# An attention and gated-unit backward kernel: dV and dK accumulated as their transposes, and one more row tile of dS turned by DMA

## The chip, the cores and the metric

The kernel runs on one core of a Trainium2 chip. The metric is the device time of one execution in microseconds (us), lower is better. Before the change it is 5135.07 us, the median of 3 runs (5125.85 to 5143.78).

## What is computed

The program computes the forward output of a small block and the gradients of all its inputs but one, in bf16. Cut to what matters (S = 2048 rows, D = 576, H = 32 heads of 128, F = 4608):

```python
xn = layernorm(x)
q  = (xn @ wq)                       # split in 32 heads
p  = softmax(q @ k_cache.T * 128**-0.5)      # per head, 2048 x 2048
s  = concat_heads(p @ v_cache) @ wo
g  = silu((sigmoid(xn @ w_gate) * (xn @ w_up)) @ w_down)
out = x + s * g
# outputs: out, and by jax.vjp with grad_out the gradients
# of x, k_cache, v_cache, wq, wo, w_gate, w_up, w_down
```

The change concerns the gradients of the two caches. Per head they are dV = P^T dO and dK = dS^T Q, with P the 2048 x 2048 matrix of softmax weights, dS = P * (dP - delta), and dP = dO V^T. Each result is 2048 x 128.

## The kernel before

The work runs in stages, one after the other on the one core.

- **Gate and up projections** (L292 to L334), **down projection** (L359 to L397): before the heads.
- **Heads** (L719 to L773): 32 heads, one after the other, with the next head's preparation woven into the present one. This is by far the longest stage.
- **Output projection** (L826 to L851): 16 row tiles, which read the heads' outputs back transposed (`oT`, L810).
- **Feed-forward gradients** (L879 to L946): 18 blocks of 256 columns. Each block loads `h_blk`, `a_blk`, `b_blk` (L865 to L873; the loads for block fb + 2 are issued in block fb), and in the first ten blocks one piece of the transposed down weights (`wdT`, L824).
- **Attention weight gradients** (L981 to L1016): 8 groups of 4 heads. Each group loads `onb` and `dqb` for the group after next (L975, L976), and the first five groups also load two pieces of the transposed up and gate weights (L1016).
- **dx** (L1032 to L1077): 8 blocks of 256 rows. Each makes 8 passes over chunks that are loaded transposed (`cf`, `cq`, L1042); three `cf` buffers and two `cq` buffers let the loads run ahead. The first block also loads the transposed `wq` (L92, called from L1044).

Inside a head the order is written by hand: every small piece of work gets a position (`at`, `anchor`, L427 to L431), a head is 64 positions long, and the pieces are issued in the order of their positions. A head has two halves of 32 positions. In the first, row tile qt (128 of the 2048 query rows, 16 tiles) gets its scores `sp` on TensorE at position 2 qt (`s_half`, L529), the softmax on VectorE and ScalarE (`sneg`, `Pq`), and then P's row tile is transposed (`trans_dma`, L584) into a `PT` tile for the product P V. In the second half, at 32 + 2 qt, the same goes for dP and dS (`dp_half`, L558; `dST` tiles for the product dS K). The products with the transposed tiles are `row_mm` (L593), 16 matmuls for each row tile, placed 12.1 positions after the start of their group of four (XO, XQ, L669). The transposed tiles come from one pool of 7 (NPT, L405).

A transpose goes one of two ways. By DMA: one `dma_start_transpose` on the SP queue for a whole 128 x 2048 row tile (L585). On TensorE: 16 transposing matmuls into PSUM and two copies, one by ScalarE and one by VectorE (`trans_pe`, L587, with `pe_transposes`, L500). `PE_DS = {9}` (L408) sends row tile 9 of dS, and no other, through TensorE. So a head issues 16 transposes of P and 15 of dS on the SP queue. That queue runs in order, and during the heads it carries almost nothing else. All other transfers of the stage (the head's K and V, its weight slices, and all results) are issued from GpSimd and go over the software queue q0.

dV and dK are made by `kv_mm` (L611). For each row tile and each 128 keys, the 128 x 128 piece of P (or dS) is the stationary operand and the row tile of dO (or Q) the moving one, 128 columns wide. The result piece has the keys in its partitions. A head makes dV and dK in two halves of 1024 keys, four passes in all. In each pass the 8 matmuls of a row tile lie at places that `level` (L692) spreads evenly over positions 24 to 86.7, given the other TensorE work (`load_`). Four pieces of 128 keys share a PSUM bank. A finished bank is copied by ScalarE and written by GpSimd's DMA directly to the output (L628 to L630), 1 KB per partition and transfer.

Of the kernel before, what the change touches and what calls it, by code (L numbers as in the profile page):

```python
# [9 lines left out]
bf = mybir.dt.bfloat16  # L10
f32 = mybir.dt.float32
PSUM = bass.MemoryType.PSUM
DRAM = bass.MemoryType.DRAM
P = 128
# [81 lines left out]
def kernel(  # L96
# [6 lines left out]
    nc = tc.nc  # L103
    cfg = dict(cfg or {})
    _, S, D = A_x.shape
    _, H, Sk, Dh = A_k_cache.shape
# [3 lines left out]
    NT = S // P  # L110
# [4 lines left out]
    CH = min(512, S)  # L115
# [18 lines left out]
    dram = ctx.enter_context(tc.tile_pool(name="dram", bufs=1, space=DRAM))  # L134
# [8 lines left out]
    dg_d = dram.tile([S, F], bf, name="dg_d")  # L143
    on2_d = dram.tile([S, HD], bf, name="on2_d")
    dq2_d = dram.tile([S, HD], bf, name="dq2_d")

    pers = ctx.enter_context(tc.tile_pool(name="pers", bufs=1))
    ident = pers.tile([P, P], bf, name="ident")
# [27 lines left out]
    with tc.tile_pool(name="pa", bufs=1) as pa:  # L176
# [159 lines left out]
        if True:  # L336
# [9 lines left out]
            with tc.tile_pool(name="a2h", bufs=1, reuse_waits="tile") as hp, \  # L346
# [12 lines left out]
                for sg in range(NT // SG):  # L359
# [7 lines left out]
                    for sl in range(SG):  # L367
# [36 lines left out]
    KPC = CH // P  # L404
    NSLAB, NPT = 20, 7  # L405
    STT2 = {4, 9, 14}
    PE_P = set()
    PE_DS = {9}  # L408
    with tc.tile_pool(name="ld2", bufs=2) as ld2, tc.tile_pool(name="ld1q", bufs=1) as ld1q, \
            tc.tile_pool(name="slab", bufs=NSLAB) as slabp, \  # L410
            tc.tile_pool(name="wsneg", bufs=2) as wsneg, \
# [15 lines left out]
        def at(pos, fn, *args):  # L427
            prog.append((pos, len(prog), fn, args))
# [179 lines left out]
            if after:  # L608
                at(pos + step * (GQ - 1) + width + AFTER, after)

        def kv_mm(bx, hs, slabs, rhs, half, qt, j, sink):  # L611
            i, jj = j // KPC, j % KPC
            if qt == 0 and jj == 0:
                bx.acc[i] = ps_acc.tile([P, KPC, P], f32, name="acckv", tag="acc")
            k0 = (half * 2 * KPC + j) * P
            nc.tensor.matmul(bx.acc[i][:, jj, :], lhsT=slabs[qt][:, k0:k0 + P], rhs=getattr(hs, rhs)[:, qt, :],  # L616
                             start=(qt == 0 and jj == 0), stop=(qt == NT - 1 and jj == KPC - 1))
            if qt == NT - 1 and jj == KPC - 1:
                sink(bx.acc[i], i)

        def kv(b, pos, hs, slabs, rhs, half, out_dram):
            ov = out_dram.rearrange("(p t) d -> p t d", t=NT)
            bx = Box()
            bx.acc = [None, None]

            def sink(acc, i):
                c = half * 2 + i
                kv_t = stg.tile([P, KPC, P], bf, name="kv")  # L628
                alt.copy(kv_t[:], acc[:], eng=KVE[i])
                nc.gpsimd.dma_start(ov[:, c * KPC:(c + 1) * KPC, :], kv_t[:])  # L630

            n = 2 * KPC
            for qt in range(NT):
                for j in range(n):
# [84 lines left out]
        for h in range(H):  # L719
            hs = Head(h)  # L720
            b = h * HEAD
            back = lambda x: b - HEAD + x if h else b - 14 + x / 8
            at(back(35.0), load_w, hs)
            at(back(35.1), load_kv, hs)
            for c in range(NCH):
                for i in range(DT):
                    at(back(QT_AT[0][c] + PSTEP * i), proj, hs, "QT", c, i, QT_AT[1])
                    at(b + DOT_AT[0][c] + PSTEP * i, proj, hs, "dOT", c, i, DOT_AT[1])
            at(b + WOT_AT, prep_wo, hs, "s")
            for g in range(2):  # L730
                at(back(KT_AT[g]), prep_kt, hs, g, KT_AT[2])
                at(b + DON_AT[g], prep_don, hs, g, DON_AT[2])
                at(b + VT_AT[g], prep_vt, hs, g, VT_AT[2])
                at(b + QN_AT[g], prep_qn, hs, g, QN_AT[2])
            for p in range(NT // 2):
                at(b + 4 * p + 2 + RINV_AT, s_rinv, hs, p)
                at(b + max(4 * p + 2.1 + RINV_AT, DON_AT[p // 4] + 0.5), s_scale, hs, p)
            for qt in range(NT):
                p1, p2 = b + 2 * qt, b + H1 + 2 * qt
                for hf in range(NHF):  # L740
                    anchor(p1 + hf, s_half, hs, qt, hf)
                    anchor(p2 + hf, dp_half, hs, qt, hf)
                at(p1 + EXP_AT, s_exp, hs, qt)
                if qt in PE_P:
                    for g in range(2):
                        at(p1 + 5.3 + g, trans_pe, hs.PT, hs.P, qt, "PT", g, "s")
                else:
                    at(p1 + PT_AT, trans_dma, hs.PT, hs.P, qt, "PT")
                if qt in PE_DS:
                    for g in range(2):  # L750
                        at(p2 + DST_PE[g], trans_pe, hs.dST, hs.dS, qt, "dST", g, "sv"[g])
                else:
                    at(p2 + DST_AT, trans_dma, hs.dST, hs.dS, qt, "dST")
            for g in range(NG):
# [21 lines left out]
    if True:  # L776
# [19 lines left out]
        with tc.tile_pool(name="c1b", bufs=1, side="right", reuse_waits="tile") as blk, \  # L796
# [26 lines left out]
            def load_wdT(i, k=0):  # L823
                nc.sync.dma_start_transpose(wdT_h[k][:, i, :], B_w_down[k * FH:(k + 1) * FH, dlo[i]:dlo[i] + P])  # L824
# [32 lines left out]
        with tc.tile_pool(name="b1o", bufs=2, reuse_waits="tile") as outp, tc.tile_pool(name="b1t", bufs=3, reuse_waits="tile") as tmpp, \  # L857
# [21 lines left out]
            for fb in range(F // FB):  # L879
# [45 lines left out]
                load_abh(fb + 2)  # L925
                if fb < DT * (NWD - 1):
                    load_wdT(fb % DT, 1 + fb // DT)
                for (blk_, out_, nm) in ((du_blk, out_7, "dwu"), (dg_blk, out_6, "dwg")):
                    stg_ = outp.tile([P, DL, FB], bf, name=nm)
                    for i, (d0, kd) in enumerate(dts[:DL]):  # L930
                        acc = psw.tile([P, 512], f32, name="accw", tag="tr")
                        for st in range(NT):
                            nc.tensor.matmul(acc[:kd, :FB], lhsT=xn_all[:, st, d0:d0 + kd], rhs=blk_[:, st, :],  # L933
                                             start=(st == 0), stop=(st == NT - 1))
                        alt.copy(stg_[:kd, i, :], acc[:kd, :FB])
                    for i, (d0, kd) in enumerate(dts[:DL]):
                        nc.gpsimd.dma_start(out_[d0:d0 + kd, fcols], stg_[:kd, i, :])
# [15 lines left out]
        HG = ldiv(H, 4)  # L953
        NHG = H // HG
        with tc.tile_pool(name="c2b", bufs=1, reuse_waits="tile") as blk, tc.tile_pool(name="c2s", bufs=2, reuse_waits="tile") as sb, \
                tc.tile_pool(name="c2w", bufs=1, reuse_waits="tile") as wp, tc.tile_pool(name="c2b0", bufs=1, reuse_waits="tile") as blk0, \
                tc.tile_pool(name="c2ps", bufs=2, space=PSUM, reuse_waits="tile") as ps, \
                tc.manual_schedule(engines={mybir.EngineType.SP}):
# [22 lines left out]
            for hg in range(NHG):  # L981
# [32 lines left out]
                load_hg(hg + 2)  # L1014
                for (dst, src, d0, kd) in wT_loads[2 * hg:2 * hg + 2]:
                    nc.sync.dma_start_transpose(dst[:, :, d0:d0 + kd], src[d0:d0 + kd, :])  # L1016

        SB2 = min(256, S)
        FC = ldiv(FT, 12)
        HC = ldiv(H, 16)  # L1020
        with tc.tile_pool(name="c4c", bufs=1, reuse_waits="tile") as chp, tc.tile_pool(name="c4s", bufs=2, reuse_waits="tile") as sb, \
                tc.tile_pool(name="c4w", bufs=1, reuse_waits="tile") as wp, \
                tc.tile_pool(name="c4ps", bufs=2, space=PSUM, reuse_waits="tile") as ps, \
                tc.manual_schedule(engines={mybir.EngineType.SP}):
# [3 lines left out]
            def load_wqT(k):  # L1028
                load_T_rows(nc, wqT_q[k], A_wq[:, k * HQ * P:(k + 1) * HQ * P], D)

            NSB = S // SB2
            for sbi in range(S // SB2):  # L1032
# [7 lines left out]
                for pi, (src_d, wT, k0, KC, nm) in enumerate(passes):  # L1040
                    ch = chp.tile([P, KC, SB2], bf, name=f"cq{pi % 2}" if nm == "cq" else f"cf{pi % 3}")
                    nc.sync.dma_start_transpose(ch[:], src_d[scol, k0 * P:(k0 + KC) * P])  # L1042
# [10 lines left out]
                for sl in range(nsl):  # L1053
# [21 lines left out]
                    dx = sb.tile([P, D], bf, name="dx")  # L1075
                    nc.vector.tensor_tensor(dx[:], t2[:], got[:], op=ALU.add)
                    (nc.sync if sbi == NSB - 1 else nc.gpsimd).dma_start(o1[rows, :], dx[:])  # L1077
        pc3.release()
        pc.release()

# [29 lines left out]
```

## Time and profile before

The profiled execution took 5140.72 us as a run, 5.7 us more than the median of the three; its span, from the first to the last instruction, is 5138.9 us. All other numbers below are from this execution.

| stage | from, us | to, us | PE busy | DMA share |
|---|---|---|---|---|
| heads (without their ends) | 480 | 3710 | 3165.43 of 3230 | 1.15 |
| feed-forward gradients | 3875 | 4460 | 582.22 of 585 | 0.73 |
| attention weight gradients | 4463 | 4714 | 251.00 of 251 | 0.81 |
| dx | 4715 | 5130 | 407.62 of 415 | 0.73 |

PE is TensorE. "Busy" is the union of the times in which an engine has an instruction under way. The DMA share is the time that packets took, summed over all queues and divided by 16 DMA engines; packets of different queues overlap on one engine, so the share can pass 1. The granted TensorE clock is 1.00 in the heads' stretch and 0.993 over the whole span.

Two more rows help later. Of the transfers, a DMA transpose of P lands 6.0 us after its issue in the median and one of dS 6.1 us; the q1 queue (SP) moved 719.49 MB in 2,626,976 packets and took 81.8% of the 16 engines' span, q0 (GpSimd) 285.79 MB and 19.4%. A head's own loads over q0 are K and V with 512 KB each, and its results 16 writes of 128 KB.

### The profile page before, as it was taken

The numbers are of one execution on the slowest core, as the hardware profiler recorded it, in microseconds if no ns is written. First come the engines' busy times: TensorE is split into PE (matmuls) and PEld (weight loads), VectorE is DVE, ScalarE is ACT, GpSimd is POOL, SyncE is SP. The second block draws the span as 40 slices with busy tenths as digits, with TensorE's granted clock in tenths as the row PEclk, the third lists the DMA queues.
The fourth block names the chain that finished last, engine by engine and source line by source line (L and its number), as shares of the span: only waits on it lengthen the run. The fifth ranks groups of instructions, "written<-read, shape, count | busy, mean of one in ns | idle before, by whom it ended". The sixth has DMA issues, their size and how long they took to land.

```text
span 5138.9 us, 128238 instructions
## 1 busy us (share of the span) xinstructions
PE 5018.4 (98%) x55312; PEld 3595.6 (70%) x55312; DVE 3072.1 (60%) x4821; ACT 2447.8 (48%) x3131; POOL 1481.5 (29%) x2197
## 2 busy tenths in 40 slices
PE   9999999999999999999999999999799999999999
PEld 3345777777777778777777877777657777754554
DVE  6546777777777788788778878877532222210101
ACT  5523656665666567666656666766401222100000
POOL 4322322332233233323323332332222333211000
PEclk9999999999999999999999999999999999999999
DMA  7887999999999999999999999999999776697775
GB/s 256 274 200 164 191 188 193 198 199 195 195 194 197 194 199 197 202 199 203 196 199 200 201 197 203 203 195 200 197 185 241 204 201 192 206 244 159 154 153 120
DMA packets 2712809, 1013.48 MB, mean 197 GB/s; under 512 B 2525744, under 2 KB 2648624, under 8 KB 2712240
## 3 DMA queue, kind: packets, MB, share of 16 engines
q1 hardware_dynamic: 2626976, 719.49, 81.8%
q0 software_dynamic: 85264, 285.79, 19.4%
q8 instruction: 432, 7.08, 0.6%
q14 instruction: 137, 1.12, 0.1%
HBM read 172.54 MB, written 201.00 MB: 73 GB/s over the span
## 4 chain that ended last, share of the span: by engine, by line
PE 90%; DMA 6%; DVE 2%; SPq 1%; ACT 1%; issue 1%; DVEq 0%; POOL 0%; ACTq 0%; POOLq 0%
PE acckv L616 16%; PE acc L597 16%; PE sp L537 8%; PE acc L1051 8%; PE dp L567 7%; PE accp L496 5%; PE accw L933 5%; DMA dST<-dSq 4%; PE dh L892 3%; PE acc L377 3%; PE accd L910 3%; PE g_ps L280 2%; PE acc L989 2%; PE acct L503 2%; PE u_ps L280 2%; PE accq L998 2%
## 5 line engine op out<-in xcount | busy, mean ns | idle before, releaser
L597 PE MATMUL acc<-Kn,dST 128*128 128x128 bf16 x8192 | 1087.1, 220 | 54.6 <-DMA dST<-dSq 54.5
L548 ACT ACTIVATE Pq<-sneg,nm 128x2048 bf16<-128x2048 bf16 x512 | 1024.7, 2001 | 227.5 <-DVE sneg L539 222.8
L616 PE MATMUL acckv<-dOn,Pq 128*128 128x128 bf16 x8192 | 1077.0, 220 | 0.0
L570 DVE SCALAR_TENSOR_TENSOR dSq<-dp,delta,Pq 128x1024 bf16<-128x1024 f32 x608 | 774.3, 1282 | 504.8 <-PE dp L567 500.6
L597 PE MATMUL acc<-Vn,PT 128*128 128x128 bf16 x8192 | 1051.5, 219 | 12.3 <-DMA PT<-Pq 12.3
L616 PE MATMUL acckv<-Qn,dSq 128*128 128x128 bf16 x8192 | 979.8, 219 | 0.0
L616 PEld LDWEIGHTS <-Pq 128*128 128x128 bf16 x8192 | 754.2, 98 | 227.8 <-issue 12.1
L616 PEld LDWEIGHTS <-dSq 128*128 128x128 bf16 x8192 | 742.8, 98 | 180.7
L597 PEld LDWEIGHTS <-dST 128*128 128x128 bf16 x8192 | 748.6, 98 | 169.8 <-DMA dST<-dSq 63.7
L597 PEld LDWEIGHTS <-PT 128*128 128x128 bf16 x8192 | 728.5, 98 | 104.4 <-DMA PT<-Pq 13.9
L539 DVE TENSOR_SCALAR_CACHE_REDUCE sneg<-sp,nm 128x1024 bf16<-128x1024 f32 x512 | 657.1, 1283 | 93.2 <-PE sp L537 66.2
L539 DVE TENSOR_SCALAR_CACHE_REDUCE sneg<-sp 128x1024 bf16<-128x1024 f32 x512 | 625.4, 1221 | 114.0 <-PE sp L537 101.0
L573 ACT ACTIVATE t<-dp,negdelta 128x1024 bf16<-128x1024 f32 x416 | 464.9, 1117 | 422.0 <-PE dp L567 415.7
L537 PE MATMUL sp<-KT,QT 128*128 128x512 bf16 x2048 | 612.0, 381 | 5.9 <-DVE sneg L539 5.6
L567 PE MATMUL dp<-VT,dOT 128*128 128x512 bf16 x2048 | 611.6, 380 | 0.0
L556 POOL TENSOR_TENSOR dOn<-dOn,rinv_all 128x256 bf16<-128x256 bf16 x256 | 153.8, 610 | 510.2 <-DVE dOn L42 323.3
L577 DVE TENSOR_TENSOR dSq<-t,Pq 128x1024 bf16<-128x1024 bf16 x416 | 289.6, 696 | 0.0
L1051 PEld LDWEIGHTS <-cf 128*128 128x128 bf16 x2304 | 146.0, 98 | 142.9 <-DMA cf<-dg_d 5.1
L496 PE MATMUL accp<-xnT,wq_h 128*128 128x512 bf16 x640 | 242.5, 384 | 2.3 <-ACT xnT L40 0.8
L933 PEld LDWEIGHTS <-xn_all 128*128 128x128 bf16 x2304 | 224.2, 98 | 27.8
L663 POOL DMA_DIRECT2D dq_d<-dq_n x128 | 99.1, 774 | 479.8 <-DVE dq_n L662 443.1
L1064 DVE SCALAR_TENSOR_TENSOR junk<-dxn,xn_all 128x576 f32<-128x576 f32 x16 | 12.1, 758 | 371.0 <-ACT dxn L1059 371.0
(185 smaller groups left out, 7044.2 us busy)
## 6 DMA issues: line engine op xcount, KB each, us to landing
out_dram<-kv POOLq DMA_DIRECT2D x256, 128.0 KB, 4.7
h_d<-h_row POOLq DMA_DIRECT2D x48, 384.0 KB, 2.8
a_d<-a_row POOLq DMA_DIRECT2D x48, 384.0 KB, 3.4
b_d<-b_row POOLq DMA_DIRECT2D x48, 384.0 KB, 4.5
a_blk<-a_d SPq DMA_DIRECT2D x18, 1024.0 KB, 5.9
b_blk<-b_d SPq DMA_DIRECT2D x18, 1024.0 KB, 21.6
du_d<-du_blk POOLq DMA_DIRECT2D x18, 1024.0 KB, 8.5
dg_d<-dg_blk POOLq DMA_DIRECT2D x18, 1024.0 KB, 11.5
```

Of the source, the lines that this page charges most:

```text
L496: nc.tensor.matmul(acc[:], lhsT=w[:, i, :], rhs=(srcT if i < DL else xnT)[:, i, cs], start=(i == 0), stop=(i == DL))
L537: nc.tensor.matmul(sp[:, c * CH:(c + 1) * CH], lhsT=hs.QT[:, qs], rhs=hs.KT[:, hf * HW_ + c * CH: hf * HW_ + (c + 1) * CH], start=True, st ...
L539: nc.vector.tensor_scalar(sneg[:, hf * HW_:(hf + 1) * HW_], sp[:], -SCALE, None if hf == 0 else nm[:, hf - 1:hf], op0=ALU.mult, op1=ALU.mi ...
L548: nc.scalar.activation(Pq[:], sneg[:], AF.Exp, bias=nm[:, hf:hf + 1], scale=-1.0, accum_out=hs.rs_all[:, qt:qt + 1])
L567: nc.tensor.matmul(dp[:, c * CH:(c + 1) * CH], lhsT=hs.dOT[:, qs], rhs=hs.VT[:, hf * HW_ + c * CH: hf * HW_ + (c + 1) * CH], start=True, s ...
L570: nc.vector.scalar_tensor_tensor(dSq[:, hsl], dp[:], hs.delta[:, qt:qt + 1], Pq[:, hsl], op0=ALU.subtract, op1=ALU.mult)
L573: nc.scalar.activation(t[:], dp[:], AF.Identity, bias=hs.negdelta[:, qt:qt + 1], scale=1.0)
L577: nc.vector.tensor_tensor(dSq[:, hsl], t[:], Pq[:, hsl], op=ALU.mult)
L597: nc.tensor.matmul(bx.acc[:, j, :], lhsT=T[qt][:, kt, :], rhs=getattr(hs, rhs)[:, kt, :], start=(kt == 0), stop=(kt == NT - 1))
L616: nc.tensor.matmul(bx.acc[i][:, jj, :], lhsT=slabs[qt][:, k0:k0 + P], rhs=getattr(hs, rhs)[:, qt, :], start=(qt == 0 and jj == 0), stop=(q ...
L933: nc.tensor.matmul(acc[:kd, :FB], lhsT=xn_all[:, st, d0:d0 + kd], rhs=blk_[:, st, :], start=(st == 0), stop=(st == NT - 1))
L1051: nc.tensor.matmul(accs[sl][j][:, :nn], lhsT=ch[:, kk, sl * P:(sl + 1) * P], rhs=w_[:, n0:n0 + nn], start=(pi == 0 and kk == 0), stop=(las ...
```

## The change

It does three things.

1. `kv_mm` swaps its operands. The row tile of dO or Q (128 x 128) is now stationary and 512 keys of P's or dS's row tile are moving. One matmul of 512 columns takes the place of four of 128. The PSUM bank then holds 128 (head dimension) x 512 (keys), which is a piece of dV or dK transposed. Two matmuls of a row tile and pass remain, at the places that the first and the fifth of the eight had.
2. The transposed pieces go, in the same 128 KB writes on GpSimd's queue, into two new scratch tensors in DRAM, `dkT_d` and `dvT_d`. A new helper `turn` later loads a head's 128 x 2048 scratch by a DMA transpose into a `turn` tile and writes that tile to the output, 4 KB per partition. There are 64 such pairs of transfers, all on the SP queue: two in each of the 18 feed-forward blocks, two in each of the 8 attention weight groups, and the last 12 in dx, one at a time. A call of `turn` first issues the writes of the tiles that the call before had loaded. Each of the three stages has a pool of two `turn` tiles of 4 KB per partition.
3. `PE_DS` is emptied: row tile 9 of dS is transposed by DMA like the others. The placing of dV and dK by `level` follows, as it no longer has to leave room for it.

```diff
+    dkT_d = dram.tile([H, P, S], bf, name="dkT_d")
+    dvT_d = dram.tile([H, P, S], bf, name="dvT_d")
+    turns = [(src[h], out[0, h].rearrange("(p t) d -> p t d", t=NT)) for h in range(H) for src, out in ((dkT_d, out_2), (dvT_d, out_3))]
+    turned = []
+
+    def turn(pool, n):
+        while turned:
+            nc.sync.dma_start(*turned.pop(0))
+        for _ in range(n):
+            if turns:
+                src, dst = turns.pop(0)
+                t_ = pool.tile([P, NT, P], bf, name="turn")
+                nc.sync.dma_start_transpose(t_[:], src)
+                turned.append((dst, t_[:]))
...
-    PE_DS = {9}
+    PE_DS = set()
...
-        def kv_mm(bx, hs, slabs, rhs, half, qt, j, sink):
-            i, jj = j // KPC, j % KPC
-            if qt == 0 and jj == 0:
-                bx.acc[i] = ps_acc.tile([P, KPC, P], f32, name="acckv", tag="acc")
-            k0 = (half * 2 * KPC + j) * P
-            nc.tensor.matmul(bx.acc[i][:, jj, :], lhsT=slabs[qt][:, k0:k0 + P], rhs=getattr(hs, rhs)[:, qt, :],
-                             start=(qt == 0 and jj == 0), stop=(qt == NT - 1 and jj == KPC - 1))
-            if qt == NT - 1 and jj == KPC - 1:
+        def kv_mm(bx, hs, slabs, rhs, half, qt, i, sink):
+            if qt == 0:
+                bx.acc[i] = ps_acc.tile([P, CH], f32, name="acckv", tag="acc")
+            k0 = (half * 2 + i) * CH
+            nc.tensor.matmul(bx.acc[i][:], lhsT=getattr(hs, rhs)[:, qt, :], rhs=slabs[qt][:, k0:k0 + CH],
+                             start=(qt == 0), stop=(qt == NT - 1))
+            if qt == NT - 1:
                 sink(bx.acc[i], i)
...
-                kv_t = stg.tile([P, KPC, P], bf, name="kv")
+                kv_t = stg.tile([P, CH], bf, name="kv")
                 alt.copy(kv_t[:], acc[:], eng=KVE[i])
-                nc.gpsimd.dma_start(ov[:, c * KPC:(c + 1) * KPC, :], kv_t[:])
+                nc.gpsimd.dma_start(dst[:, c * CH:(c + 1) * CH], kv_t[:])
...
-                for j in range(n):
-                    at(b + pos[qt * n + j], kv_mm, bx, hs, slabs, rhs, half, qt, j, sink)
+                for i in range(2):
+                    at(b + pos[qt * n + i * KPC], kv_mm, bx, hs, slabs, rhs, half, qt, i, sink)
...
-                kv(b, pv, hs, hs.P, "dOn", half, out_3[0, h])
-                kv(b, pk_, hs, hs.dS, "Qn", half, out_2[0, h])
+                kv(b, pv, hs, hs.P, "dOn", half, dvT_d[h])
+                kv(b, pk_, hs, hs.dS, "Qn", half, dkT_d[h])
...
                 load_abh(fb + 2)
                 if fb < DT * (NWD - 1):
                     load_wdT(fb % DT, 1 + fb // DT)
+                turn(tkp, 2)
...
                 for (dst, src, d0, kd) in wT_loads[2 * hg:2 * hg + 2]:
                     nc.sync.dma_start_transpose(dst[:, :, d0:d0 + kd], src[d0:d0 + kd, :])
+                turn(tkp, 2)
+            turn(tkp, 0)
...
                     if sbi == 0 and pi in (1, 3, 4, 6):
                         load_wqT((1, 3, 4, 6).index(pi))
+                    elif sbi and pi % 3 == 1:
+                        turn(tkp, 1)
```

The feed-forward stage and dx end with a `turn(tkp, 0)` too, which only writes what is still held.

More of the change, by code (lines that the diff above doesn't have):

```diff
@@ L609, in rows, with kv @@
                 at(pos + step * (GQ - 1) + width + AFTER, after)
-        def kv_mm(bx, hs, slabs, rhs, half, qt, j, sink):
-            i, jj = j // KPC, j % KPC
-            if qt == 0 and jj == 0:
-                bx.acc[i] = ps_acc.tile([P, KPC, P], f32, name="acckv", tag="acc")
-            k0 = (half * 2 * KPC + j) * P
-            nc.tensor.matmul(bx.acc[i][:, jj, :], lhsT=slabs[qt][:, k0:k0 + P], rhs=getattr(hs, rhs)[:, qt, :],
-                             start=(qt == 0 and jj == 0), stop=(qt == NT - 1 and jj == KPC - 1))
-            if qt == NT - 1 and jj == KPC - 1:
+        def kv_mm(bx, hs, slabs, rhs, half, qt, i, sink):
[5 more added lines that the diff above has]
+            if qt == NT - 1:
                 sink(bx.acc[i], i)
-        def kv(b, pos, hs, slabs, rhs, half, out_dram):
-            ov = out_dram.rearrange("(p t) d -> p t d", t=NT)
+        def kv(b, pos, hs, slabs, rhs, half, dst):
             bx = Box()
@@ L856 @@
         FB = min(256, F)
-        with tc.tile_pool(name="b1o", bufs=2, reuse_waits="tile") as outp, tc.tile_pool(name="b1t", bufs=3, reuse_waits="tile") as tmpp, \
+        with tc.tile_pool(name="b1o", bufs=2, reuse_waits="tile") as outp, tc.tile_pool(name="b1k", bufs=2, reuse_waits="tile") as tkp, tc.tile_pool(name="b1t", bufs=3, reuse_waits="tile") as tmpp, \
                 tc.tile_pool(name="b1r", bufs=2, reuse_waits="tile") as dblk, \
@@ L955 @@
         with tc.tile_pool(name="c2b", bufs=1, reuse_waits="tile") as blk, tc.tile_pool(name="c2s", bufs=2, reuse_waits="tile") as sb, \
+                tc.tile_pool(name="c2k", bufs=2, reuse_waits="tile") as tkp, \
                 tc.tile_pool(name="c2w", bufs=1, reuse_waits="tile") as wp, tc.tile_pool(name="c2b0", bufs=1, reuse_waits="tile") as blk0, \
@@ L1016 @@
                     nc.sync.dma_start_transpose(dst[:, :, d0:d0 + kd], src[d0:d0 + kd, :])
+                turn(tkp, 2)
+            turn(tkp, 0)
         SB2 = min(256, S)
@@ L1021 @@
         with tc.tile_pool(name="c4c", bufs=1, reuse_waits="tile") as chp, tc.tile_pool(name="c4s", bufs=2, reuse_waits="tile") as sb, \
+                tc.tile_pool(name="c4k", bufs=2, reuse_waits="tile") as tkp, \
                 tc.tile_pool(name="c4w", bufs=1, reuse_waits="tile") as wp, \
@@ L1077 @@
                     (nc.sync if sbi == NSB - 1 else nc.gpsimd).dma_start(o1[rows, :], dx[:])
+            turn(tkp, 0)
+            assert not turns
         pc3.release()
```

## The prediction, made before the changed kernel had run

> **What bounds the kernel now.** I read the page first: busy shares, slices and the chain of waits.
>
> ```profile
> PE 5018.4 (98%) x55312; PEld 3595.6 (70%) x55312; DVE 3072.1 (60%) x4821; ACT 2447.8 (48%) x3131; POOL 1481.5 (29%) x2197
> DMA  7887999999999999999999999999999776697775
> PE 90%; DMA 6%; DVE 2%; SPq 1%; ACT 1%; issue 1%; DVEq 0%; POOL 0%; ACTq 0%; POOLq 0%
> ```
>
> TensorE looks like the bound, but the DMA row is at 9 in all slices of the heads. So I asked how close the second one is. First TensorE's need, from the chain in order of time, whose rows (start, us, what) give real pitches, since the 219 ns and 380 ns of the groups are overlapping durations:
>
> ```profile
> 3597.01 0.43 PE sp L537 x2
> 3689.80 0.45 PE acct L503 x8
> 3725.68 4.91 PE acckv L616 x88
> ```
>
> 512 columns take 0.43 / 2 = 0.215 us; 128 columns take 4.91 / 88 = 0.0558 us, and a transpose 0.45 / 8 = 0.056. Per head (the counts of the groups divided by 32) there are 168 matmuls of 512 columns (64 sp, 64 dp, 40 accp) and 1109 of 128 (512 each at L597 and L616, 85 transposes): 36.1 + 61.9 = 98.0 us. In the trace the calmest heads follow each other in 99.0 us; the mean is higher. The score tiles' first matmul starts at 471.1 and their last at 3649.2, 31.5 heads later: 3178.1 / 31.5 = 100.9 us.
>
> Then the SP queue. Its timeline in a calm head (start, us, what):
>
> ```profile
> 2417.63 32.15 SPq L585 DMA_TRANSPOSE PT<-Pq  x11
> 2449.89 49.13 SPq L585 DMA_TRANSPOSE dST<-dSq  x15
> 2499.11 21.61 SPq L585 DMA_TRANSPOSE PT<-Pq  x6
> ```
>
> and the rows of its line, with minimum, median and maximum ns of one:
>
> ```profile
> L585 SPq DMA_TRANSPOSE PT<-Pq x512: 1316/3028/8442, 478.4 to 3656.1; - x171
> L585 SPq DMA_TRANSPOSE dST<-dSq x480: 1316/3080/8579, 524.2 to 3713.3; - x160
> ```
>
> 2449.89 + 49.13 = 2499.02, and the next issue begins at 2499.11: the queue is never free. Over the stage 992 issues fill 478.4 to 3713.3, 3.26 us each, 31 x 3.26 = 101.1 us per head. Is it busy or waiting? The wait view puts most of its time down to dp matmuls (L567), for which a transpose of P or dS has no use. In the head at 2800 to 2900 the trace has row tile 4 of dS finished on VectorE at 2857.0 and its issue begun at 2865.0; over the stage an issue begins 2 to 9 us after its data are there, and ends when the transfer before it has landed. So it is the transfers that take 3.26 us, not their producers. The heads have two bounds within 2%, and where TensorE waits it is for `dST` (54.5 us before L597, 12.3 for `PT`).
>
> **The change, part by part.** *kv_mm*, per head: 512 x 0.0558 = 28.6 us become 128 x 0.215 = 27.5: 1.05 us less. *Row tile 9 on TensorE*: 16 x 0.056 = 0.9 us less, and a ScalarE copy of 1.02 and a VectorE copy of 0.68 that other work hid. TensorE's need falls to 96.1, some 97.1 with the calm head's 1.0 of small waits; 32 x 1.95 = 62 us if TensorE decided. Copies, sizes and queue of the results stay, so they cost nothing new.
>
> *Row tile 9 on the SP queue*: one issue more, 32 per head. Queued behind it are row tiles 10 to 15 and the next head's P; `row_mm` waits for them, and behind it in TensorE's order everything else. Price: the trace has no idle queue during heads, so I bound it. Above, the mean of its neighbours, 3.26 us, which includes what q0's traffic (K, V, results) takes from them; that traffic does not grow. Below, transposes from DRAM in dx, where little else runs:
>
> ```profile
> 4764.49 10.31 SPq L1042 DMA_TRANSPOSE cf<-du_d  x3
> 4806.22 10.92 SPq L1042 DMA_TRANSPOSE cf<-du_d  x3
> ```
>
> 3.44 us for 256 x 1536 elements is 2.3 us for 128 x 2048. I take 2.5, nearer to the row without other traffic. The calm heads show that the queue can do its 31 in 99.0 us, 2 less than its mean, and part of these 2 may be room that the other heads need for their bursts or may be free; I take 0.5 off, with bounds 0 and 2. So a head grows by 2.0 us, and TensorE's 1.95 us go into waiting: 32 x 2.0 = +64. Bounds: 32 x (2.3 - 2.0) = 10 and 32 x 3.26 = 104.
>
> The Trainium skill, "DMA: Bandwidth & Descriptors", section "Latency and other measured facts", gives a DMA transpose an effective 261 GB/s; 524 KB would then take an estimated 2.0 us and 32 of them 64 us per head. This trace does not agree (3.26 us, 161 GB/s); what the time would be by it is the first rival below.
>
> *The 64 turns.* A pair is two transposes (2.3 to 3.3 each) and two writes of 512 KB. Bounds for a write: four 2 MB loads at L975 and L976 land about 7 us apart, 1.8 per 512 KB; V's 512 KB land 5.4 us after issue. A pair is 8 to 17 us; I take 11, with the waits for landings between. Feed-forward blocks are 32.5 us long and loads run a block ahead:
>
> ```profile
> 4050.67 1.79 SPq L872 DMA_DIRECT2D b_blk<-b_d  x1
> 4052.52 17.91 SPq L824 DMA_TRANSPOSE wdT<-in_B_w_down_dram  x1
> 4082.72 0.36 SPq L872 DMA_DIRECT2D a_blk<-a_d  x1
> ```
>
> From 4070.4 to 4082.7 the queue is free, 12.3 us: 11 fit behind the loads, cost 0. (At 17 the ten blocks with `wdT` fall 5 behind each, 47 less the lead of about 30: 17.) In the attention weight groups less is free:
>
> ```profile
> 4620.76 16.26 SPq L1016 DMA_TRANSPOSE wgT_sb<-in_B_w_gate_dram  x2
> 4637.12 0.53 SPq L975 DMA_DIRECT2D onb<-on_d  x1
> 4651.81 0.37 SPq L976 DMA_DIRECT2D dqb<-dq_d  x1
> 4683.27 6.90 SPq L1042 DMA_TRANSPOSE cf<-du_d  x2
> 4714.74 3.35 SPq L1042 DMA_TRANSPOSE cf<-du_d  x1
> ```
>
> A group is 31.5 us, and after `onb` (landed some 9 us later) about 5 us are free. Groups 1 to 4 add 11 each and find 5 three times: the queue leaves group 4 at 4637 + 44 - 14 = 4667. The last two loads of 7 to 9 us end at 4684, before the 4699 at which group 7 needs `dqb`. Then three pairs stand ahead of dx: 4717, and the last two writes; `cf` begins at 4719 in place of 4683.3. TensorE wants it at 4714.7, and the first dx block, whose loads (64 us of queue, mostly 20 pieces of `wq`) already made it wait until 4767.0, gets its last chunk at about 4783. Cost 15; 0 if a pair takes 8, 30 if 17. The later dx blocks have 15 us free each (4817 to 4832) for one and a half pairs: 0, at most 15 if chunks land late.
>
> *Sum*, against the profiled run: 5140.7 + 64 + 15 = 5219.7; the median stands 5.7 lower, so **5214 us**. The likeliest case's own range: 5135 + 10 = 5145 to 5135 + 104 + 45 = 5284.
>
> **The rivals.** *A. TensorE decides, faster.* The transfers stretch to fill the time there is, and go quicker when more are wanted. For it: calm heads run at TensorE's pace, and single issues took 1316 ns. Against it: row tiles of dS wait 5 to 9 us in the queue and TensorE still stops for them; if they could go quicker they would. It decides in the heads if a piece takes under 97.1 / 32 = 3.03 us with the traffic beside it, against 3.26 now. Time: 5135 - 62 + 15 = 5088. *B. No difference.* The queue has the full 2 us of room and the price is 2.3: +10 in the heads, 0 behind: 5145. *C. The last stages starve.* A pair costs 17, and row tile 9 its full 3.26: 5135 + 104 + 17 + 30 + 15 = 5301. It decides from a pair over about 13 us on (12.3 free in a feed-forward block). For it: `b_blk` takes 20 us to land already, beside writes on q0. Against it: those loads are needed a block later. That the change is not in the program is excluded: its listing has 16 dS transposes per head, 128 `acckv` matmuls and 64 turns.
>
> **How the numbers follow.** The forecast has 0.72, A 0.13, B 0.08, C 0.07. The three runs lie within 0.35%, so 0.3% (15 us) is about what can be told from no change. Faster by more is A alone: 0.13. Within is B: 0.08. Slower is the rest: 0.79. The range goes into A's upper part (PE deciding with part of the stalls kept) and to C's lower end: 5115 to 5285; what is left out is most of A and of C, under 0.2.
>
> **What would show it.** In the profile after: 512 dS issues at L585 without gaps, a mean of about 3.2 us, and idle time before L597 grown from 54.5 to some 180 us for `dST` (4 us per head); TensorE's busy share of the heads down; `acckv` with 4096 matmuls of 512 columns at 0.215 us; in the last groups, turns ahead of the first `cf`, and a first dx block that ends some 15 us later in its stage. It is wrong if heads follow each other in under 100 us, if issues begin when their data are ready, or if the first `cf` lands before 4714.7's counterpart.

## The result, and the profile after

The changed kernel takes 5197.24 us, the median of 4 runs (5166.02 to 5208.78), against 5134.45 us (4 runs) for the kernel before on the same chip: ratio 1.0116, 95% interval 1.0084 to 1.0148. It is slower, 17 us under the forecast. The profiled execution took 5200.65 us, its span is 5198.5 us. First the page of the kernel after: busy times, the slices, the chain of waits and the two groups of `row_mm`.

```profile
PE 4979.1 (96%) x42512; PEld 3038.2 (58%) x42512; DVE 3066.7 (59%) x4789; ACT 2414.2 (46%) x3099; POOL 1483.2 (29%) x2197
...
DMA  7877999999999999999999999999999999999995
...
PE 74%; DMA 21%; DVE 2%; ACT 1%; issue 1%; SPq 1%; DVEq 0%; ACTq 0%
...
L612 PE MATMUL acc<-Kn,dST 128*128 128x128 bf16 x8192 | 996.1, 220 | 76.8 <-DMA dST<-dSq 75.8
...
L612 PE MATMUL acc<-Vn,PT 128*128 128x128 bf16 x8192 | 957.1, 220 | 71.0 <-DMA PT<-Pq 70.3
```

TensorE has less to do (4979.1 us after 5018.4) in a longer span, and the chain that ends last now goes through DMA for 21% of the span where it was 6%. Its waits (L612 now) are no longer for `dST` alone: 75.8 us for it (54.5 before) and 70.3 for `PT` (12.3 before). The DMA row stays at 9 to the last slice but one: the 64 turns fill the last stages.

The SP queue in one head (start, us, what), then the row of the dS transposes:

```profile
2404.94 52.78 SPq L600 DMA_TRANSPOSE PT<-Pq  x16
2457.83 51.75 SPq L600 DMA_TRANSPOSE dST<-dSq  x16
2509.69 21.52 SPq L600 DMA_TRANSPOSE PT<-Pq  x6
```

```profile
L600 SPq DMA_TRANSPOSE dST<-dSq x512: 1316/3082/8235, 520.8 to 3748.4; - x171
```

2404.94 + 52.78 = 2457.72, and the next issue starts at 2457.83: no gap, 104.6 us for 32 pieces in this head. (A piece is one such transpose of a row tile.) Over the stage 1024 issues follow each other every 3.198 us (3.26 before, for 992). An issue starts after its data are there by 6.3 us in the median for P and 8.2 us for dS; before it was 3.8 and 6.1.

Where the 59.6 us of span went, by stage. A stage lasts from its first matmul to the first matmul of the next (the feed-forward from its first `accd` matmul, dx to its last matmul); a head from its first exponential to that of the next head. The last two columns are experiments told below.

| us | before | after | turns taken out | turns placed lighter |
|---|---|---|---|---|
| a head, mean of 31 | 100.50 | 101.67 | 102.67 | 101.43 |
| feed-forward | 587.8 | 604.3 | 583.1 | 587.7 |
| attention weights | 251.7 | 254.0 | 251.7 | 251.7 |
| dx | 417.0 | 421.6 | 417.2 | 418.1 |

So 36 of the 59.6 us (31 x 1.17) come from the heads, 16.5 from the feed-forward, 2.3 and 4.6 from the last two stages; the output projection takes 2.2 more, the start 1.6 less. Each column is one profiled execution. The heads of the last three columns are the same program but for what happens after them, so 101.43 to 102.67 is how far a head's mean moves from one execution to the next. The window of after for the feed-forward (window, length, busy PE, PEld, DVE, ACT, POOL, granted clock, DMA share, GB/s):

```profile
3911.00:4510.00 599.00, 587.10 (x5450) 466.71 (x5447) 160.03 (x405) 127.73 (x260) 178.00 (x268) 0.99 1.10 259
```

The DMA share is 1.10 (0.73 before), and TensorE is busy 587 of 599 us. The SP queue there:

```profile
3987.94 14.49 SPq L158 DMA_TRANSPOSE turn<-dkT_d  x1
4002.48 9.66 SPq L158 DMA_TRANSPOSE turn<-dvT_d  x1
...
4027.65 1.00 SPq L153 DMA_DIRECT2D out_dram<-turn  x2
4048.12 3.16 SPq L158 DMA_TRANSPOSE turn<-dkT_d  x1
```

A block of 32.5 us issues two turns, which take 14.49 and 9.66 us here. From 4028.65 to 4048.12 it stands still, 19.5 us: there are two `turn` tiles, and the next turn needs the tile whose write, issued at 4027.65, lands at 4048.10. That landing took 20.5 us where the median of these writes is 5.2, and the write was not alone: the `wdT` issued at 4014.84 lands at 4046.00, 31 us later, and most of the transfers then under way land between 4046 and 4051. The window of the time between (columns as above):

```profile
4030.00:4040.00 10.00, 10.00 (x108) 8.77 (x107) 1.27 (x3) 1.12 (x3) 1.61 (x3) 1.00 1.17 56
```

The DMA engines are as busy as ever (share 1.17) and move 56 GB/s, where the whole stage has 259. I call this a crawl. Counted in steps of 2.5 us with a share over 0.9 and under 110 GB/s, crawls add up to 42 us in the feed-forward of this trace and to none in that of before.

From there the loads run late, and TensorE (start, us, what, idle before it and its releaser) stops in a block and again at the stage's end:

```profile
4111.81 3.57 PE L905 MATMUL dh<-wdT,doBT 128*128 128x256 bf16 x16 [5.81 <-DMA wdT<-in_B_w_down_dram]
```

```profile
4515.62 4.55 PE L1005 MATMUL acc<-ds_all,onb 128*128 128x512 bf16 x23 [7.57 <-DMA onb<-on_d]
```

### The profile page after: what moved, and what is told of

It reads as the page before. It is cut to its first block, busy times and chain, and to the rows that moved or that the text cites. A ratio compares the mean times of both kernels' runs of the same rounds, so it can differ in the third digit from the quotient of the medians.

```text
span 5198.5 us, 102786 instructions
## 1 busy us (share of the span) xinstructions
PE 4979.1 (96%) x42512; PEld 3038.2 (58%) x42512; DVE 3066.7 (59%) x4789; ACT 2414.2 (46%) x3099; POOL 1483.2 (29%) x2197
## 4 chain that ended last, share of the span: by engine, by line
PE 74%; DMA 21%; DVE 2%; ACT 1%; issue 1%; SPq 1%; DVEq 0%; ACTq 0%
PE acc L612 13%; PE acckv L630 12%; DMA dST<-dSq 9%; DMA PT<-Pq 8%; PE acc L1072 7%; PE dp L582 6%; PE sp L552 5%; PE accw L947 4%; PE accp L511 4%; PE dh L905 3%; PE acc L392 3%; PE accd L923 3%; PE acc L1005 2%; PE g_ps L295 2%; PE u_ps L295 2%; PE accq L1014 2%
## 5 line engine op out<-in xcount | busy, mean ns | idle before, releaser
L612 PE MATMUL acc<-Kn,dST 128*128 128x128 bf16 x8192 | 996.1, 220 | 76.8 <-DMA dST<-dSq 75.8
L612 PE MATMUL acc<-Vn,PT 128*128 128x128 bf16 x8192 | 957.1, 220 | 71.0 <-DMA PT<-Pq 70.3
L612 PEld LDWEIGHTS <-dST 128*128 128x128 bf16 x8192 | 696.7, 98 | 528.9 <-DMA dST<-dSq 125.0
L612 PEld LDWEIGHTS <-PT 128*128 128x128 bf16 x8192 | 683.6, 98 | 506.3 <-DMA PT<-Pq 110.6
L630 PE MATMUL acckv<-Pq,dOn 128*128 128x512 bf16 x2048 | 761.3, 380 | 0.0
L630 PE MATMUL acckv<-dSq,Qn 128*128 128x512 bf16 x2048 | 760.0, 381 | 0.0
L630 PEld LDWEIGHTS <-dOn 128*128 128x128 bf16 x2048 | 200.6, 98 | 79.0 <-issue 0.7
L630 PEld LDWEIGHTS <-Qn 128*128 128x128 bf16 x2048 | 201.3, 98 | 74.6 <-issue 1.9
```

Source lines behind the costliest of these rows:

```text
L612: nc.tensor.matmul(bx.acc[:, j, :], lhsT=T[qt][:, kt, :], rhs=getattr(hs, rhs)[:, kt, :], start=(kt == 0), stop=(kt == NT - 1))
L630: nc.tensor.matmul(bx.acc[i][:], lhsT=getattr(hs, rhs)[:, qt, :], rhs=slabs[qt][:, k0:k0 + CH], start=(qt == 0), stop=(qt == NT - 1))
```

## The experiments

Each was run beside the kernel before, so ratios are compared. They came in three groups; the medians of before were 5128.9, 5123.5 and 5133.0.

**Row tile 9 alone on the queue.** The kernel before with one line changed:

```diff
-    PE_DS = {9}
+    PE_DS = set()
```

> The kernel before with one edit: row tile 9 of dS goes by DMA (PE_DS empty); no swapped operands, no turns. Queue theory (in the heads the SP queue's transposes set the pace, so a 32nd one lengthens each head whatever TensorE saves): heads 101.7 us on average as in the changed kernel (before: 100.5), time 5134 + 37 = 5171 (5150 to 5190). Operand theory (the 512-wide dV/dK matmuls disturb TensorE's order, row tile 9 costs nothing): heads 100.5 or less, time 5134 or less.

5206.14 us (4 runs), ratio 1.0157 (1.0118 to 1.0195), heads 102.75 apart, 2.25 more. The direction is the queue's; the size is larger than expected, 77 us or 2.4 per head. TensorE has less to do here and waits more for `dST`. The row of the dS tiles that says what TensorE waited for:

```profile
  DMA dST<-dSq: 194.8, 177
```

That is the idle time of matmuls and weight loads together before this tile, with its number of waits; before it was 118.2 us in 65.

But the edit is not a clean one: `PE_DS` also goes into `level`, so the dV and dK matmuls move. The row of their accumulators (`acckv`) for what was waited for has

```profile
  ACT kv L40: 32.4, 30
```

In 30 heads TensorE stops 1.08 us for ScalarE's copy of a `kv` bank, about 1.05 per head. No such stop is in the trace of before or in any version with swapped operands. How much of the 77 us it makes was not separated; the price of row tile 9 therefore rests on the other pair of kernels, told below.

**The swap and the turns, without row tile 9.** The changed kernel with `PE_DS = {9}`.

> The changed kernel with one edit: row tile 9 of dS is transposed on TensorE as before (PE_DS = {9}); swapped operands and turns stay. Queue theory: 31 pieces in the queue, TensorE 1.05 us per head faster: heads 99.5 (98.2 to 100.5), which gives 32 us, later stages 24 us longer than before: 5127 (5100 to 5150). Operand theory: heads stay near 101.7, time near 5190.

5109.46 us (10 runs), ratio 0.9954 (0.9927 to 0.9980): faster than before, by more than was expected. Heads are 98.93 apart, and the calm ones 97.9. So taking 1.05 us per head from TensorE was worth something even though the queue had its 31 pieces as before, and that with turns that cost as in the changed kernel. (The profiled execution, 5132 us, is the slowest of the ten; its feed-forward has 628.5 us, with 67 us of crawls.)

**No turns.** The changed kernel without its 64 turns (`turn(tkp, 2)` goes in both stages); the outputs dK and dV are not written.

```diff
-                turn(tkp, 2)
...
-                    elif sbi and pi % 3 == 1:
-                        turn(tkp, 1)
```

> The changed kernel without the 64 turns: dK and dV stay transposed in the scratch, those two outputs are not written. Both theories of the heads: heads as in the changed kernel, 101.7. If the turns cost what the two traces differ by behind the heads (16.5 us in the feed-forward gradients, 2.3 and 4.6 in the two stages after it): 5197 - 23 = 5174 (5160 to 5185), feed-forward stage 588 us. If that difference is chance: 5197, feed-forward stage about 600.

5169.29 us (6 runs), ratio 1.0087 (1.0055 to 1.0119): the turns cost 28 us by the medians (5197.24 - 5169.29) and 15 by the ratios, whose intervals overlap, so the times alone do not settle it; the rest of the loss stays. The stages do: without turns the feed-forward takes 583.1 us, the last two 251.7 and 417.2, which is 21, 2.3 and 4.4 less than with them.

**No turns and no writes of dK and dV.** The one before, and the 8 writes of 128 KB per head left out too:

```diff
-                nc.gpsimd.dma_start(dst[:, c * CH:(c + 1) * CH], kv_t[:])
```

> As the kernel without turns, and the heads' 8 writes of 128 KB of dV and dK are left out too, so neither is written anywhere: 1 MB less per head on the software queue, nothing changed on the SP queue. Queue theory, with transposes slowed by what else the DMA engines move (in the trace of before, landings follow each other by 2.3 us where under 10 KB of other data moved and by 5.5 us where over 400 KB did): heads fall to TensorE's pace, 97.1 to 98.5, time 5174 - 32 x 3.9 = 5050 (5030 to 5090). If a transpose takes its 3.2 us whatever else moves: heads stay at 101.7, time 5174. Operand theory: 5174 too.

5057.14 us (4 runs), ratio 0.9861 (0.9817 to 0.9904): 112 us less than with the writes, 3.5 per head, though SP issues the same 32 pieces. Its SP queue in a head:

```profile
2411.42 49.67 SPq L600 DMA_TRANSPOSE dST<-dSq  x16
2461.20 49.01 SPq L600 DMA_TRANSPOSE PT<-Pq  x16
```

98.7 us for the 32; over the stage a piece takes 3.09 us, and 3.23 with the writes. The median head is 97.37 and 20 of the 30 heads after the first lie within 0.4 of it: there TensorE decides, although the queue has no gap (the mean is 98.39). So what a piece costs is not the queue's own: it depends on GpSimd's traffic. And a queue without gaps is not by itself the bound.

**One piece more.** The changed kernel, with row tile 9 of dS transposed a second time into a tile that nobody reads:

```diff
+                if qt == 9:
+                    at(p2 + DST_AT, extra, hs.dS, qt)
```

> The changed kernel with row tile 9 of dS transposed twice: one more piece of 512 KB per head on the SP queue into a tile that nobody reads, 33 pieces in place of 32; TensorE's work is that of the changed kernel. Queue theory: every piece on SP pushes what stands behind it, whoever reads it, by the 2.3 us that row tile 9 alone cost, or up to the 3.2 us that a piece takes in the changed kernel: heads 101.7 + 2.3 to 3.2 = 104.0 to 104.9 us apart, time 5197 + 32 x (2.3 to 3.2) = 5271 to 5299. If the price is what the changed kernel's profile alone showed, 1.2 us: 5235. Rival, the late operand: what slowed the heads is that row_mm of row tile 9 now waits for a landing, not the queue's length: unchanged, 5197 within 15.

5289.9 us (4 runs), ratio 1.0318 (1.0276 to 1.0360), heads 104.92 apart: 3.25 more than in the changed kernel. Its SP queue:

```profile
2422.20 34.21 SPq L600 DMA_TRANSPOSE dST<-dSq  x10
2456.50 3.99 SPq L604 DMA_TRANSPOSE xT<-dSq  x1
2460.59 17.82 SPq L600 DMA_TRANSPOSE dST<-dSq  x6
```

The 33rd piece (`xT`) has no reader and no producer of its own, yet costs its full 3.2 us, by the ratios too (1.0318 - 1.0116, some 104 us or 3.2 per head): pieces follow each other every 3.200 us, with 32 or with 33 of them. The late operand of row tile 9 is excluded as the cause, and in the heads of the changed kernel a piece more on the queue counts in full. That TensorE's load counts for nothing there is not shown: row tile 9 alone and the changed kernel have the same 32 pieces, and the one without the swap, with its stops for `kv`, is slower.

**Writes of the turned tiles from GpSimd.** The version with row tile 9 on TensorE, and in `turn`:

```diff
-            nc.sync.dma_start(*turned.pop(0))
+            nc.gpsimd.dma_start(*turned.pop(0))
```

> The changed kernel with row tile 9 back on TensorE (the version that came out at 5109), and the 64 writes of turned tiles issued from GpSimd in place of SP. Theory, SP is held up: what the turns cost after the heads is time in which the SP queue waits for a turned tile to land before it can issue its write and the next load; then the feed-forward falls back from 604 to 628 us to under 595 and the boundary stall (7.7 us for onb) goes: 5109 - 15 to 30 = 5080 to 5095. Rival, the DMA engines are full: the transfers themselves (64 MB in all through the turns) stretch the loads, whoever issues them: feed-forward still 604 to 628, time 5100 to 5115. Worse is possible too, to 5125, where GpSimd's own results wait behind the landing.

5142.82 us (10 runs), ratio 1.0037 (1.0009 to 1.0066): worse than either theory; the third case of the expectation has a mechanism, not the size. TensorE no longer stops for any load of SP there; it stops for about 22 us in the feed-forward (614.7 us) and 21 in the attention weight groups (281.6 us) for copies of results. Another 8 to 9 us in each stage are not stops: TensorE is busy 591.5 and 260.1 us, where the version told next takes 582.6 and 251.7 for the same work, at a granted clock of 0.98 and 0.97 against 1.00. Why the clock was lower was not tested.

In the groups the third case holds. GpSimd stands, mostly 6 to 7 us, at the write of a turned tile until the turn has landed; the writes of `dwq` are issued behind it and land, mostly, 7 to 8 us later, and the next copies into these tiles, with TensorE behind them, wait for that.

In the feed-forward it is mostly otherwise. GpSimd's queue, a stop of TensorE, the landing of the two `dwd` writes before it (window 4195:4233) and the window:

```profile
4229.02 0.54 POOL L153 DMA_DIRECT2D out_dram<-turn  x1 [25.08 <-DMA turn<-dkT_d]
```

```profile
4232.82 3.57 PE L947 MATMUL accw<-du_blk,xn_all 128*128 128x256 bf16 x16 [5.14 <-DVE dwu L42]
```

```profile
DMA to landing us min/median/max: 26.6/27.7/28.8
```

```profile
4215.00:4230.00 15.00, 12.68 (x109) 8.26 (x107) 2.84 (x7) 1.38 (x3) 0.98 (x2) 0.99 1.27 65
```

GpSimd stands 25.08 us at the write of a turned tile, 229.0 us over the stage. But VectorE's copies before this stop wait for two writes of `dwd` that GpSimd had issued ahead of its wait, at 4201.13 and 4202.84. They took 26.6 and 28.8 us to land, in a crawl (65 GB/s at a share of 1.27); before, the median of these writes is 11.3. Three of the four stops are of this kind. So the edit moved the wait for a landing to another queue, where it stops the groups, and did not free SP: a turn still needs a tile whose write has landed, and SP stands some 100 us before its turns in the feed-forward, with either queue for the writes. The crawls of that stage, 62 us here, stayed too. Whether the traffic of the turns alone makes them is open.

**Fewer turns in the blocks that load `wdT`.** The version with row tile 9 on TensorE, SP writes, and:

```diff
-                turn(tkp, 2)
+                turn(tkp, 1 if fb < 6 else 2)
```

The rest falls into dx, where 6 more slots are used.

> The changed kernel with row tile 9 back on TensorE, and the turns placed otherwise: one in each of the first 6 feed-forward blocks (which also load 18 us of wdT) and two in the other 12, two in each attention weight group, 18 in dx where DMA was at a share of 0.87: 30 + 16 + 18 = 64. SP writes, as in the changed kernel. Theory, the feed-forward is short of queue time in the blocks with wdT alone: the wdT stalls (6 us and 5 us) go, the rest stays: 5109 - 5 to 15 = 5094 to 5104. Rival, the loss sits at the boundary and in the blocks with two turns: no change, 5109 within 10.

5091.34 us (7 runs), ratio 0.9926 (0.9902 to 0.9951), 38 us under before by the ratio, and with the last one below the fastest that computes everything. It is at the good end of its theory: not the `wdT` stalls alone are gone, but also the one at the boundary. Its window of the feed-forward:

```profile
3829.00:4412.00 583.00, 582.45 (x5443) 464.99 (x5442) 160.38 (x405) 127.45 (x260) 177.03 (x266) 1.00 0.95 258
```

TensorE is busy 582.45 of 583 us, at a DMA share of 0.95. The later blocks still have their two turns each, and cost nothing: with the early blocks relieved, crawls are down to 5 us and a turn takes 3.1 us on average, where it was 6.5 in the feed-forward of the changed kernel. Over all traces, the four versions with two turns in every block (the changed kernel, the swap without row tile 9, one piece more, writes from GpSimd) have 42 to 68 us of crawls in the feed-forward, all others at most 15. What makes them is not shown.

**Both edits together.** Writes from GpSimd and the lighter placing, row tile 9 on TensorE.

> Both edits together: row tile 9 on TensorE, writes of the turned tiles from GpSimd, and one turn in each of the first 6 feed-forward blocks, the rest in dx. If SP being held up and the blocks with wdT are two causes, the gains add: 5070 to 5090, feed-forward near 585. If both act on the same stall: as the better of the two alone. If the DMA engines are full: 5100 to 5115.

5119.36 us (10 runs), ratio 0.9993 (0.9973 to 1.0014), outside all three cases. Feed-forward 583.3, attention weight groups 285.7: the lighter place helps, the writes from GpSimd still block the groups. The gains do not add; one of them was none.

**The changed kernel with lighter turns.** All 32 pieces on the queue, the same placing.

> The changed kernel itself (row tile 9 on the SP queue, 32 pieces per head), its turns placed as in the version that came out at 5091: one in each of the first 6 feed-forward blocks, two in the other 12, 16 in the attention weight groups, 18 in dx. Theory, the turns cost by their place alone: the feed-forward falls from 604 to about 583, the boundary stall for onb goes, heads stay 101.7 apart: 5197 - 21 - 2 to 5 = 5169 to 5174, as with no turns at all (5169). Rival, the queue time of the turns only moves on to dx: feed-forward 583 but dx longer by as much, 5190 to 5200.

5169.43 us (9 runs), ratio 1.0075 (1.0055 to 1.0095), as expected and as with no turns at all. So the turns are free by their place, and what remains against the version at 5091 is row tile 9: 1.0075 / 0.9926 = 1.0150, some 77 us, 2.4 per head. Against row tile 9 alone (1.0157), which has the same 32 pieces, the swap gains 42 us; in part that is the stop for `kv`, which this version does not have. Its SP queue in the feed-forward:

```profile
4020.69 0.98 SPq L153 DMA_DIRECT2D out_dram<-turn  x1
4021.77 7.81 SPq L158 DMA_TRANSPOSE turn<-dvT_d  x1
4034.52 0.36 SPq L885 DMA_DIRECT2D a_blk<-a_d  x1
```

4021.77 + 7.81 = 4029.58, and `a_blk` follows at 4034.52: the queue has 5 us to spare in the block, and no write's landing is waited for.

**A piece less than before.** The version at 5091 with row tiles 9 and 14 of dS on TensorE, 30 pieces on SP.

```diff
-    PE_DS = {9}
+    PE_DS = {9, 14}
```

> The version that came out at 5091 (kv_mm swapped, row tile 9 of dS on TensorE, turns placed lighter), with row tile 14 of dS put on TensorE too: 30 pieces per head on SP, 16 more transposes of 0.056 = 0.9 us per head on TensorE. If at 31 pieces TensorE already decides most heads (their floor there was 97.9): floor 98.8, mean 98.9 to 99.3, no gain: 5085 to 5105. If the queue still decides (31 x 3.2 = 99.2): 30 x 3.2 = 96 frees it, and the mean falls to the floor, at most 0.4 under the present 99.2: 5075 to 5085. If a piece off the queue were worth its 3.2 us however few are left: 5091 - 32 x 2.3 = 5017, which TensorE's need excludes.

5091.82 us (4 runs), ratio 0.9924 (0.9902 to 0.9946): no gain, as the first case has it. Its SP queue now has gaps:

```profile
2419.54 47.08 SPq L600 DMA_TRANSPOSE dST<-dSq  x14
2469.37 51.19 SPq L600 DMA_TRANSPOSE PT<-Pq  x16
```

2419.54 + 47.08 = 2466.62, and the next issue is at 2469.37; over the stage some 440 us of such gaps, 14 per head, where versions with 31 to 33 pieces have 120 to 130 in all. Heads are 99.77 apart, and 29 of the 30 after the first lie within 0.4 of 99.89: at 30 pieces TensorE decides. Its floor is 2 us above the 97.9 of 31 pieces, twice what was expected: 0.9 us are the added transposes, and 0.8 are stops before them for copies of other tiles (`woT_h`, `dq_n`); the rest is not accounted for. So this version does not say what a piece less is worth by itself.

## Why the prediction was right, and where not

**The bound.** Right. The forecast said that the SP queue was full and that a 32nd piece would move everything behind it. The 33rd piece (+3.25 us per head) shows it, and so do the writes left out (-3.5 with the same pieces). What it had named as signs held: 512 dS issues without gaps, 3.198 us each, heads more than 100 us apart, `acckv` as 4096 matmuls of 512 columns that start 0.216 us after each other. One did not: the idle time was to be 180 us for `dST`; it is 75.8 for `dST` and 70.3 for `PT`, 146 in all. The backlog does not end with dS, it runs into the next head's P.

**Row tile 9.** This term was +64 and should have been +77: 2.4 us per head by the times of the two versions with the swap and the lighter turns (32 pieces against 31), 2.23 by the heads of their profiles. The pair without the swap gives the same 77, with the stops for `kv` in it. The price of 2.5 us looks good, but not for the reason given: on the queue a piece costs 3.2 us, as the 33rd shows, so the upper bound of 3.26 was the right one, and the 0.5 us taken off for room was not there. That the pair has 2.4 and not 3.2 fits the 0.9 us that row tile 9 no longer costs TensorE, which the forecast had put at nothing; no run tests this 0.9 alone.

**The swap.** This step failed: its 1.05 us per head were put at nothing, because the queue was to hide them. The version with swap, 31 pieces and lighter turns is 38 us faster than before (ratio 0.9926), 1.2 per head. The queue has no gaps in either trace, yet TensorE decides in half of the heads: of the 30 after the first, 15 lie within 0.4 us of 99.03 before, and the others, which wait for a transpose, average 102.2. With the swap 15 lie within 0.4 of 97.87 and the others average 100.8. Both kinds got shorter: two bounds so close are not a maximum. Why the heads that wait got shorter too was not taken apart.

The errors of these two terms have opposite signs: +64 was forecast for the heads, +77 - 38 = +39 is what the versions give, and +36 is what the profile has. The turns err the other way again, as follows, so that the total came within 17 us is in part luck.

**The turns.** Forecast: 0 in the feed-forward, 15 at the boundary to dx. Measured: 28 us by the medians, against the lighter placing as against no turns (by the ratios 21 and 15, which the intervals hardly tell from nothing); in the profiles 16.5 more than before in the feed-forward, its boundary stall included, 2.3 in the groups, 4.6 in dx. The step that failed is "11 fit behind the loads, cost 0". A pair holds the queue for about 11 us in the attention weight groups, just the 11 of the forecast, but for some 19 in the first blocks of the feed-forward, more than the bound of 17: a transpose takes 6.3 us on average there, and the queue then waits 2.6 to 19.5 us for a tile whose write must land. With 12.3 us free in a block with `wdT`, each falls 7 behind. The lead of about 30 us that the forecast had counted is gone after some four blocks, and TensorE first stops at 4078, in the sixth. The formula for the upper bound was the right one; the price put into it was too low, as the longest of these pairs fall in crawls, which the trace of before does not have.

**The boundary to dx.** In after the turns stand ahead of the first `cf`, as forecast. The SP queue and TensorE there:

```profile
4759.49 2.71 SPq L153 DMA_DIRECT2D out_dram<-turn  x2
4762.25 7.56 SPq L1061 DMA_TRANSPOSE cf<-du_d  x2
```

```profile
4769.58 11.93 PE L1072 MATMUL acc<-wuT_sb,cf 128*128 128x512 bf16 x96 [0.69 <-DMA cf<-du_d]
4785.37 5.00 PE L1072 MATMUL acc<-wuT_sb,cf 128*128 128x512 bf16 x27 [3.85 <-DMA cf<-du_d]
```

`cf` begins 7.4 us ahead of the stage's first matmul, where it was 31 before, and TensorE stops only 0.69 and then 3.85 us for it. The forecast had the first block end 15 us later; its last chunk lands 57.0 us into the stage (4826.6 - 4769.6), before it was 52.4 (4767.0 - 4714.6): 4.6 later, and the stage grew by as much. What the step overlooked stood in its own rows: the third `cf` of before is issued at 4714.74, though the issue before it ended at 4697.7. For 17 us the queue had stood still until the stage began; that hole took up most of the delay.

**The rivals.** Times near that of A, TensorE decides (5088), came only where traffic was taken away (5057) or where the queue kept its 31 pieces (5091). Its condition was a piece under 3.03 us; with all writes in place a piece takes 3.198. The Trainium skill, "DMA: Bandwidth & Descriptors", section "Latency and other measured facts", has an effective 261 GB/s for a DMA transpose with a non-contiguous middle dimension. The trace does not agree: it has 524 KB in 3.198 us, 164 GB/s, in a stage where all traffic together is 200 GB/s. No difference (5145) is outside what was measured. The last stages did starve, as the third rival had it, though for 28 us at most and not for 62.

## What to carry to other kernels

Where two bounds lie within 2% of each other, put neither at nothing: here relief on the one was worth about its size (1.2 us per head for 1.05) and load on the other three quarters of its own or more (2.4 and 3.2 for a piece of 3.2). Cost the parts of a change apart, as a gain (the swap, -38 us) may ride with a loss (row tile 9, +77) that is a one-line choice. A queue that runs in order has room only until it must wait for a landing: cost a pair "load, then write from the same buffer" with both landings and the buffer's return, block by block, and put such work where the queue has time to spare. Read GB/s beside the DMA share: a high share at a low rate marks a time in which every transfer lands late. Moving the waiting instruction to another queue helps only if nothing that matters stands behind it there.

## What the runs showed of the hardware

A DMA transpose of 512 KB has no one price. In the trace of before, those landings between which the other queues together moved under 10 KB follow each other every 2.3 us, those with 400 to 2000 KB between them every 5.5 us; in the changed kernel it is 2.4 and 5.4. A line through all of them rises by about 0.005 us per KB of other traffic and explains a third of their spread. The version without the writes of dK and dV agrees roughly: 1 MB less per head on GpSimd's queue made a head 3.5 us shorter by the times, at the same 32 pieces. So writes that nobody waits for set the pace of the heads through what the two queues share; whether that is the DMA engines or the memory behind them, no run separates.

In the feed-forward with two turns in every block there are crawls of 5 to 20 us, in which DMA is busy (share 1.17 and 1.27 in the two windows shown) and moves 56 and 65 GB/s in place of some 260; writes and loads that fall into them took 20 to 31 us to land. What brings them on is open.
